# Linear attention's running state in a fused attention, FFN and expert kernel: summed in SBUF by VectorE, or summed in PSUM from keys that are scaled beforehand

## The chip, the cores and the metric

The kernel runs on one core of one Trainium2 chip. Its time is device microseconds from launch to end; the lower the better. Three runs of the kernel before gave 433.2, 433.91 and 435.3 us, median 433.91.

## The reference

Three stages follow one another, for two batches of 768 tokens. The first is attention with a decaying state, per batch and for each of 8 heads of 64 columns:

```
gamma[h] = 1 - 2 ** (-5 - h)
state = gamma * state + outer(k[t], v[t])        # 64 x 64 per head
y[t]  = q[t] @ state / 8
```

The second stage is a gated FFN with a convolution over three tokens (512 to 1024 to 512 columns). The third routes every token to one of 8 experts and applies that expert's two matrices. All of it is float32.

## The kernel before

Attention works on chunks of 128 tokens, six per head (`NCH = 6`, chunks 0 to 5), and on two heads at a time. Such a pair is a `Head` object: j = 0 lies on partitions 0 to 63, j = 1 on 64 to 127. There are 8 pairs, 0 to 7, so 48 steps. The order of instructions is the order of the Python program on each engine; no scheduler moves them.

One step calls `scores(c)` for one chunk and `output(c)` for the chunk two steps earlier. In TensorE's order a step is:

- `s_ps` (L279): the keys of the chunk against the queries of both heads; VectorE multiplies it by the decay mask into `at` (L281).
- `inc` (L287): keys times values of the chunk, 128 x 128, for chunks 0 to 4. It has one PSUM buffer. VectorE turns it into the next state `st` on the two diagonal 64 x 64 blocks: a copy for chunk 0 (L292), and for the others `new = gamma ** 128 * old + inc` (L294), one instruction per head.
- `y` (L297, L299): the chunk's own part from `at` and the values `vz`, and for chunks 1 to 5 the state's part, from `st` and the scaled queries. It has two PSUM buffers. ScalarE rounds `y` to the high part of `xT` (L301), VectorE writes the rest as the low part (L302), one step later.

Each float32 matmul is two instructions in the trace (x2). After these, `advance()` lets a few generators run one piece each on ScalarE, VectorE and GpSimd:

- `prepare()` of the next pair starts two steps after a pair's first: ScalarE copies the queries into `qz` (L250, two halves), GpSimd scales the queries in place (L253), ScalarE scales the keys in place by `gamma ** (127 - t)`, one instruction per head (L260), and copies the values into `vz` (L274). For pair 0, which is loaded and prepared in two parts, VectorE does one head's share (L248, L258).
- `convert()` turns the FFN's weights, which come as 64-bit words, into float32 high and low parts: L149 and L150 on VectorE, L151 on ScalarE, an add on GpSimd (L153), the high part on ScalarE (L171), the low part on GpSimd or VectorE (L173). For the second matrix it also transposes on TensorE and makes a small product (`wt`, `wc`, L186 to L192). A buffer of raw words comes free when L153 has read it; SyncE issues all loads in one queue (L143 for these words, L230 to L235 for a pair).

From step 25 on `ffn_in` slices (L133 to L135, 128 x 384) are put between attention's steps, 0.7 per step, and `hidden()` follows them on ScalarE and VectorE (L347 to L354). Attention takes from the start to about 90 us of the span; then come the rest of the FFN, the routing (about 210 to 240 us) and the experts.

Of the kernel before, what the change touches and what calls it, by code (L numbers as in the profile page):

```python
# [9 lines left out]
F32 = mybir.dt.float32  # L10
# [13 lines left out]
P = 128  # L24
CH = 128
# [16 lines left out]
A_COLS = 3 * CH + 2  # L42
# [12 lines left out]
def constants():  # L55
# [4 lines left out]
    for h in range(H):  # L60
        c, j = a[:, h // 2], h % 2
        c[:, C_DM + j * CH:C_DM + (j + 1) * CH] = np.where(d >= 0, 0.125 * g[h] ** np.maximum(d, 0), 0.0)
        c[:, C_KD + j] = g[h] ** (CH - 1 - t)
        c[64 * j:64 * j + 64, C_QD:C_QD + CH] = 0.125 * g[h] ** (t + 1)
# [27 lines left out]
def tile_kernel(ctx, tc, cat, cst, qT, kT, kN, vN, w_in, conv_w, w_out, wg, w1, w2, out):  # L92
# [125 lines left out]
    class Head:  # L218
# [21 lines left out]
        def prepare(self):  # L240
            hp = self.hp
            qd = ca[:, hp, C_QD:C_QD + CH]
            for c in self.parts:
                t = slice(c.start * CH, c.stop * CH)
                for j in range(2):
# [5 lines left out]
                    yield 1  # L251
                q1 = self.q1[:, c.start:c.stop]
                po.tensor_tensor(out=q1, in0=q1, in1=qd.unsqueeze(1).to_broadcast([P, len(c), CH]), op=ALU.mult)  # L253
                for j in range(2):
                    k1 = self.kv[:, 0, c.start:c.stop, 64 * j:64 * j + 64]
                    kd = ca[:, hp, C_KD + j:C_KD + j + 1]
                    if len(self.parts) > 1 and j:
                        ve.tensor_scalar(out=k1, in0=k1, scalar1=kd, scalar2=None, op0=ALU.mult)  # L258
                    else:
                        se.activation(out=k1, in_=k1, func=AF.Copy, scale=kd)  # L260
                    if len(self.parts) > 1:
                        self.values(c, j)
                    yield 1

            if len(self.parts) == 1:
                yield 1
                for c in (range(3), range(3, 6)):
                    for j in range(2):
                        self.values(c, j)
                    yield 3  # L270
# [12 lines left out]
        def output(self, c):  # L283
            at = self.at.pop(c)
            if c + 1 < NCH:
                inc = ps1.tile([P, P], F32, tag="i", name="inc", bufs=1)
                te.matmul(inc, self.kv[:, 0, c, :], self.kv[:, 1, c, :], start=True, stop=True)  # L287
                old, new = self.st[c % 2], self.st[(c + 1) % 2]
                for j in range(2):
                    pj = slice(64 * j, 64 * j + 64)  # L290
                    if c == 0:
                        ve.tensor_copy(out=new[pj, pj], in_=inc[pj, pj])  # L292
                    else:
                        ve.scalar_tensor_tensor(out=new[pj, pj], in0=old[pj, pj], scalar=self.g[j] ** CH, in1=inc[pj, pj], op0=ALU.mult, op1=ALU.add)  # L294
# [765 lines left out]
```

## Time and profile before

| | us |
|---|---|
| median of three runs | 433.91 |
| the profiled execution | 433.53 |
| its span, first to last instruction | 431.8 |
| TensorE busy in the span | 406.7 (94%) |
| VectorE busy | 290.1 (67%) |
| ScalarE busy | 259.4 (60%) |
| GpSimd busy | 91.6 (21%) |

Times in rows are microseconds from the start of the span. PE is TensorE, PEld its weight loads, DVE is VectorE, ACT is ScalarE, POOL is GpSimd, SP is SyncE. "x2" behind a row of the timeline means that two such instructions follow one another and are merged. What stands in brackets behind a row is the engine's idle time before it, and what ended that.

### The profile page before, as it was taken

The page shows a single profiled execution, that of the slowest core. Times are in us where ns is not written, and L with a number is a line of the kernel's source. Part 1 is how long each engine was busy: PE and PEld are TensorE (multiplying, and loading weights), DVE is VectorE, ACT ScalarE, POOL GpSimd, SP SyncE. Part 2 cuts the span into 40 slices and gives each one's busy share as a digit, 9 for nine tenths or more (in the row PEclk, how much of TensorE's full clock was granted, in tenths as well). Part 3 has the DMA queues.
Part 4 walks back from the last instruction along what each step waited for, and adds up shares of the span by engine and source line. Part 5 has one row for each costly group of instructions (what it writes and reads, how often), then busy time and mean ns, then how long its engine had stood idle before and what let it go on. Part 6 is the DMA issues. An engine that isn't in the chain of part 4 may idle for free.

```text
span 431.8 us, 7294 instructions
## 1 busy us (share of the span) xinstructions
PE 406.7 (94%) x2412; PEld 327.2 (76%) x2412; DVE 290.1 (67%) x518; ACT 259.4 (60%) x429; POOL 91.6 (21%) x92
## 2 busy tenths in 40 slices
PE   8898999997999999999999899999989999999991
PEld 7787897896898778989768676867738676776881
DVE  3798789798766350477899057968663796858650
ACT  2787677666755212566604166869555786958560
POOL 5256664213000000000000330205212132111210
PEclk9999999999999999999999999999999999999997
DMA  7989773320000101000296999999979999675001
GB/s 239 380 289 399 257 218 87 96 92 1 2 2 0 49 29 46 26 0 2 82 355 214 358 382 350 347 385 407 379 272 330 393 367 362 266 257 205 34 26 37
DMA packets 27324, 86.59 MB, mean 201 GB/s; under 512 B 3598, under 2 KB 4622, under 8 KB 27280
## 3 DMA queue, kind: packets, MB, share of 16 engines
q1 hardware_dynamic: 25200, 79.76, 50.6%
q0 software_dynamic: 2080, 6.29, 3.8%
q8 instruction: 21, 0.34, 0.3%
q14 instruction: 23, 0.19, 0.1%
HBM read 105.18 MB, written 6.55 MB: 259 GB/s over the span
## 4 chain that ended last, share of the span: by engine, by line
PE 35%; issue 26%; DMA 18%; DVE 14%; ACT 3%; POOL 2%; SPq 0%; POOLq 0%; DVEq 0%
DMA out_dram<-yo,it 15%; PE h_ps L133 5%; PE h_ps L135 4%; PE h_ps L134 4%; PE x_ps L133 4%; PE x_ps L134 3%; PE x_ps L135 3%; PE y L297 3%; PE s_ps L279 3%; DVE cc L350 2%; DMA kv<-in_kN_dram 2%; DVE na L149 2%; PE inc L287 2%; DVE na L150 1%; PE y L299 1%
## 5 line engine op out<-in xcount | busy, mean ns | idle before, releaser
L133 PE MATMUL h_ps<-xT,wih 128*128 128x384 f32 x128 | 46.5, 363 | 2.3 <-ACT wc L192 2.3
L350 DVE SCALAR_TENSOR_TENSOR cc<-h,cw,cc 128x768 f32<-128x768 f32 x32 | 35.1, 1097 | 16.8 <-ACT cc L347 16.8
L860 POOL DMA_INDIRECT out_dram<-yo,it x13 | 16.7, 1283 | 137.1 <-ACT yo L859 137.1
L724 POOL DMA_INDIRECT xg<-xs,it x13 | 18.8, 1442 | 125.5 <-DMA qc<-in_w_dram 118.6
L134 PE MATMUL h_ps<-xT,wih 128*128 128x384 f32 x128 | 43.1, 337 | 0.0
L135 PE MATMUL h_ps<-xT,wil 128*128 128x384 f32 x128 | 43.1, 336 | 0.0
L133 PE MATMUL x_ps<-woh,hg 128*128 128x512 f32 x96 | 38.5, 401 | 0.0
L134 PE MATMUL x_ps<-wol,hg 128*128 128x512 f32 x96 | 37.5, 391 | 0.0
L135 PE MATMUL x_ps<-woh,hg 128*128 128x512 f32 x96 | 37.5, 390 | 0.0
L715 DVE TENSOR_TENSOR ws0l<-r,ws0l 128x1024 fp32r<-128x1024 f32 x22 | 26.0, 1222 | 16.3 <-ACT ws0l L714 16.1
L297 PE MATMUL y<-at,vz 128*128 128x128 f32 x192 | 30.6, 281 | 1.7 <-DMA kv<-in_kN_dram 0.9
L715 DVE TENSOR_TENSOR ws0h<-r,ws0h 128x1024 fp32r<-128x1024 f32 x22 | 26.0, 1222 | 8.3 <-ACT ws0h L714 8.2
L715 DVE TENSOR_TENSOR wc<-r,wc 128x1024 fp32r<-128x1024 f32 x22 | 25.9, 1221 | 7.9 <-ACT wc L714 7.9
L714 ACT ACTIVATE ws0l<-r 128x1024 fp32r<-128x1024 f32 x22 | 22.1, 1052 | 13.6 <-PE y L135 13.6
L153 POOL TENSOR_TENSOR na<-na,raw 128x512 int32<-128x512 int32 (+1 forms) x17 | 21.9, 1290 | 38.2 <-DVE na L150 12.6
L715 DVE TENSOR_TENSOR ws1h<-r,ws1h 128x1024 fp32r<-128x1024 f32 x22 | 26.0, 1222 | 6.0 <-ACT ws1h L714 4.0
L279 PE MATMUL s_ps<-qz,kq 128*128 128x256 f32 x96 | 29.0, 384 | 1.0 <-DVE qz L248 1.0
L714 ACT ACTIVATE wc<-r 128x1024 fp32r<-128x1024 f32 x22 | 22.1, 1054 | 11.3 <-PE g L135 11.3
L297 PEld LDWEIGHTS y<-at,vz 128*128 128x128 f32 x192 | 25.3, 191 | 4.3 <-DVE xT L302 2.3
L133 PEld LDWEIGHTS h_ps<-xT,wih 128*128 128x128 f32 x128 | 24.1, 188 | 5.5 <-ACT wc L192 2.6
L281 DVE TENSOR_TENSOR at<-s_ps,ca 128x256 f32<-128x256 f32 x48 | 20.2, 420 | 11.6 <-PE s_ps L279 11.5
L486 ACT ACTIVATE xn<-x_ps 128x512 f32<-128x512 f32 x10 | 6.0, 599 | 32.8 <-PE x_ps L135 15.5
(231 smaller groups left out, 1041.5 us busy)
## 6 DMA issues: line engine op xcount, KB each, us to landing
r<-in_w_dram SPq DMA_DIRECT2D x88, 512.0 KB
qc<-in_w_dram SPq DMA_DIRECT2D x32, 512.0 KB
qs1l<-in_w_dram SPq DMA_DIRECT2D x32, 512.0 KB
raw<-in_w_in_dram SPq DMA_DIRECT2D x8, 512.0 KB
raw<-in_w_out_dram SPq DMA_DIRECT2D x8, 512.0 KB
kq<-in_qT_dram SPq DMA_DIRECT2D x7, 384.0 KB
kq<-in_kT_dram SPq DMA_DIRECT2D x7, 384.0 KB
kv<-in_vN_dram SPq DMA_DIRECT2D x7, 384.0 KB
```

The lines of the kernel that those rows point to most:

```text
L133: te.matmul(ps, lhi, rhi, start=first, stop=False)
L134: te.matmul(ps, lhi, rlo, start=False, stop=False)
L135: te.matmul(ps, llo, rhi, start=False, stop=last)
L153: po.tensor_tensor(out=a, in0=a, in1=lo, op=ALU.add)
L279: te.matmul(ps, self.kq[:, 0, tok], self.qz[:, :, tok], start=True, stop=True)
L281: ve.tensor_tensor(out=self.at[c], in0=ps, in1=self.dm, op=ALU.mult)
L297: te.matmul(y, vz[:, c, j, :], at[:, j, :], start=(j == 0), stop=(c == 0 and j == 1))
L350: ve.scalar_tensor_tensor(out=cc, in0=h[:, i:i + S], scalar=cw[:, m, i:i + 1], in1=cc, op0=ALU.mult, op1=ALU.add)
L714: se.activation(out=w[:, 0, h, :], in_=r, func=AF.Copy)
L715: ve.tensor_tensor(out=w[:, 1, h, :], in0=r, in1=w[:, 0, h, :].bitcast(F32), op=ALU.subtract)
L724: return po.indirect_dma_start(out=xg, out_offset=None, in_=xs[0:n], in_offset=bass.IndirectOffsetOnAxis(ap=it[:, j:j + 1], axis=0), bound ...
L860: po.indirect_dma_start(out=out, out_offset=bass.IndirectOffsetOnAxis(ap=it[:, j:j + 1], axis=0), in_=yo, in_offset=None, bounds_check=NT ...
```

## The change

The decay between chunks is moved from the state into the keys. The factor of a key becomes `gamma ** (127 - t + 128 * (4 - n))` for chunk n of 0 to 4, so that the plain sum of the chunks' `inc` products is the state, up to the factor `gamma ** (128 * (c + 1 - 5))` after chunk c.

- The keys of all five chunks and both heads are scaled by one GpSimd multiplication (128 x 640, its second operand a table broadcast over each head's 64 columns), ahead of the scaling of the queries. The last chunk's keys are no longer scaled. The two ScalarE instructions per pair (L260), and VectorE's two for pair 0 (L258), are gone. The table grows from 386 to 394 columns.
- `inc` is one PSUM tile per pair to which every chunk's product is added (`start=(c == 0)`).
- After each product ScalarE copies the first head's block of the sum into `st` times its factor, and VectorE the second head's. The two VectorE instructions (L292, L294) are gone.

```diff
--- before.py
+++ after.py
@@ -39,7 +39,8 @@
 
 
 C_DM, C_QD, C_KD = 0, 2 * CH, 3 * CH
-A_COLS = 3 * CH + 2
+NST = NCH - 1
+A_COLS = 3 * CH + 2 * NST
 
 C_ID = 0
 C_S0 = C_ID + P
@@ -60,7 +61,8 @@
     for h in range(H):
         c, j = a[:, h // 2], h % 2
         c[:, C_DM + j * CH:C_DM + (j + 1) * CH] = np.where(d >= 0, 0.125 * g[h] ** np.maximum(d, 0), 0.0)
-        c[:, C_KD + j] = g[h] ** (CH - 1 - t)
+        for n in range(NST):
+            c[:, C_KD + 2 * n + j] = g[h] ** (CH - 1 - t + CH * (NST - 1 - n))
         c[64 * j:64 * j + 64, C_QD:C_QD + CH] = 0.125 * g[h] ** (t + 1)
     c = np.zeros((P, C_COLS))
     e = np.arange(E)
@@ -249,21 +251,20 @@
                     else:
                         se.activation(out=self.qz[pj, j, t], in_=self.kq[pj, 1, t], func=AF.Copy)
                     yield 1
+                n = min(c.stop, NST)
+                k1 = self.kv[:, 0, c.start:n, :].rearrange("p c (j d) -> p (c j) d", j=2)
+                kd = ca[:, hp, C_KD + 2 * c.start:C_KD + 2 * n].unsqueeze(2).to_broadcast([P, 2 * (n - c.start), D])
+                po.tensor_tensor(out=k1, in0=k1, in1=kd, op=ALU.mult)
                 q1 = self.q1[:, c.start:c.stop]
                 po.tensor_tensor(out=q1, in0=q1, in1=qd.unsqueeze(1).to_broadcast([P, len(c), CH]), op=ALU.mult)
-                for j in range(2):
-                    k1 = self.kv[:, 0, c.start:c.stop, 64 * j:64 * j + 64]
-                    kd = ca[:, hp, C_KD + j:C_KD + j + 1]
-                    if len(self.parts) > 1 and j:
-                        ve.tensor_scalar(out=k1, in0=k1, scalar1=kd, scalar2=None, op0=ALU.mult)
-                    else:
-                        se.activation(out=k1, in_=k1, func=AF.Copy, scale=kd)
-                    if len(self.parts) > 1:
+                if len(self.parts) > 1:
+                    for j in range(2):
                         self.values(c, j)
+                        yield 1
+
+            if len(self.parts) == 1:
+                for _ in range(3):
                     yield 1
-
-            if len(self.parts) == 1:
-                yield 1
                 for c in (range(3), range(3, 6)):
                     for j in range(2):
                         self.values(c, j)
@@ -283,15 +284,13 @@
         def output(self, c):
             at = self.at.pop(c)
             if c + 1 < NCH:
-                inc = ps1.tile([P, P], F32, tag="i", name="inc", bufs=1)
-                te.matmul(inc, self.kv[:, 0, c, :], self.kv[:, 1, c, :], start=True, stop=True)
-                old, new = self.st[c % 2], self.st[(c + 1) % 2]
-                for j in range(2):
-                    pj = slice(64 * j, 64 * j + 64)
-                    if c == 0:
-                        ve.tensor_copy(out=new[pj, pj], in_=inc[pj, pj])
-                    else:
-                        ve.scalar_tensor_tensor(out=new[pj, pj], in0=old[pj, pj], scalar=self.g[j] ** CH, in1=inc[pj, pj], op0=ALU.mult, op1=ALU.add)
+                if c == 0:
+                    self.sum = ps1.tile([P, P], F32, tag="i", name="inc", bufs=1)
+                te.matmul(self.sum, self.kv[:, 0, c, :], self.kv[:, 1, c, :], start=(c == 0), stop=True, skip_group_check=True)
+                new = self.st[(c + 1) % 2]
+                d = [g ** (CH * (c + 1 - NST)) for g in self.g]
+                se.activation(out=new[0:64, 0:64], in_=self.sum[0:64, 0:64], func=AF.Copy, scale=d[0])
+                ve.tensor_scalar(out=new[64:128, 64:128], in0=self.sum[64:128, 64:128], scalar1=d[1], scalar2=None, op0=ALU.mult)
             y = ps1.tile([P, CH], F32, tag="y", name="y")
             for j in range(2):
                 te.matmul(y, vz[:, c, j, :], at[:, j, :], start=(j == 0), stop=(c == 0 and j == 1))
```

TensorE's order is the same in both programs. Three places in the order of the other engines follow; line numbers are each program's own, and the brackets name the engines and DMA queues whose semaphores an instruction waits for.

First, ScalarE where pair 3 begins: high part of pair 2's last chunk, a weight conversion (`wih`, `raw`) and the queries of pair 4 (`qz_104`). In the kernel before these rows stand there:

```order
L311 ACTIVATE cw<-na 128x24 [waits Pool_49]
L301 ACTIVATE xT<-y 128x128 [waits PE_49]
L171 ACTIVATE wih<-na 128x512 [waits Pool_49]
L151 ACTIVATE raw<-raw 128x512 [waits DMAHW6_49,DVE_49,Activation_49]
L250 ACTIVATE qz_104<-kq 64x768 [waits DMAHW7_49]
L301 ACTIVATE xT<-y 128x128 [waits PE_49]
L250 ACTIVATE qz_104<-kq 64x768
```

Here no copy into the state is ScalarE's. In the changed kernel ScalarE has these rows there:

```order
L310 ACTIVATE cw<-na 128x24 [waits Pool_49]
L300 ACTIVATE xT<-y 128x128 [waits PE_49]
L173 ACTIVATE wih<-na 128x512 [waits Pool_49]
L153 ACTIVATE raw<-raw 128x512 [waits DMAHW6_49]
L252 ACTIVATE qz_104<-kq 64x768 [waits DMAHW7_49]
L292 ACTIVATE st_110<-inc 64x64 [waits PE_49]
L300 ACTIVATE xT<-y 128x128 [waits PE_49]
L252 ACTIVATE qz_104<-kq 64x768
```

The copies of `inc` into `st` stand behind the conversion and the queries and ahead of the high parts.

The rows of VectorE at the same place in the kernel before, with the conversion (`na`) and the masked scores (`at`):

```order
L313 CAST sel<-cs 40x10
L281 TENSOR_TENSOR at<-s_ps,ca 128x256 [waits PE_49]
L302 TENSOR_TENSOR xT<-y,xT 128x128 [waits Activation_49]
L149 TENSOR_SCALAR na<-raw 128x512 [waits DMAHW6_49,Pool_49]
L150 SCALAR_TENSOR_TENSOR na<-raw,na 128x512 [waits DVE_49]
L281 TENSOR_TENSOR at<-s_ps,ca 128x256 [waits PE_49]
L292 COPY st_110<-inc 64x64 [waits PE_49]
L292 COPY st_110<-inc 64x64
```

Here two copies follow `at`, one per head, and wait for TensorE alone. In the changed kernel VectorE has these:

```order
L312 CAST sel<-cs 40x10
L282 TENSOR_TENSOR at<-s_ps,ca 128x256 [waits PE_49]
L301 TENSOR_TENSOR xT<-y,xT 128x128 [waits Activation_49]
L151 TENSOR_SCALAR na<-raw 128x512 [waits DMAHW6_49,Pool_49]
L152 SCALAR_TENSOR_TENSOR na<-raw,na 128x512 [waits DVE_49]
L282 TENSOR_TENSOR at<-s_ps,ca 128x256 [waits PE_49]
L293 TENSOR_SCALAR st_110<-inc 64x64 [waits Activation_49]
```

The copy of the sum (`st<-inc`) waits for ScalarE, where the copies before waited for TensorE; behind it stand the low part (`xT`) and the next `at`.

Second, ScalarE where pair 7 begins, around the table load for the sigmoid (`cc`). In the kernel before:

```order
L352 ACT_TABLE_LOAD
L352 ACTIVATE cc<-cc 128x768 [waits DVE_49]
L301 ACTIVATE xT<-y 128x128 [waits PE_49]
L186 ACTIVATE wt<-wt_ps 128x512 [waits Pool_49]
L171 ACTIVATE woh<-na 128x512 [waits Pool_49]
L301 ACTIVATE xT<-y 128x128 [waits PE_49] x2
```

Here the high parts of pair 6's last chunk and of pair 7's first two chunks follow with nothing of the state between them. In the changed kernel ScalarE has these:

```order
L351 ACT_TABLE_LOAD
L351 ACTIVATE cc<-cc 128x768
L300 ACTIVATE xT<-y 128x128 [waits PE_49]
L188 ACTIVATE wt<-wt_ps 128x512 [waits Pool_49]
L173 ACTIVATE woh<-na 128x512 [waits Pool_49]
L292 ACTIVATE st_110<-inc 64x64 [waits PE_49]
L300 ACTIVATE xT<-y 128x128 [waits PE_49]
L292 ACTIVATE st_109<-inc 64x64 [waits PE_49]
L300 ACTIVATE xT<-y 128x128 [waits PE_49]
```

The first copy of pair 7 stands behind the table load, the sigmoid, a high part and two pieces of the conversion (`wt`, `woh`).

Third, GpSimd in pairs 1 and 2: the queries (`kq`) of pairs 2 and 3, low parts of weights (`wil`) and the conversion's adds (`na`). In the kernel before:

```order
L253 TENSOR_TENSOR kq<-kq,ca 128x768 [waits DMAHW4_49,DMAHW2_49,Activation_49]
L173 TENSOR_TENSOR wil<-na,wih 128x512 [waits Activation_49]
L153 TENSOR_TENSOR na<-na,raw 128x512 [waits DMAHW7_49,DVE_49,Activation_49]
L253 TENSOR_TENSOR kq<-kq,ca 128x768 [waits DMAHW1_49,DMAHW0_49,DMAHW3_49,PE_49,Activation_49]
L153 TENSOR_TENSOR na<-na,raw 128x24 [waits DMAHW0_49,DVE_49,Activation_49]
```

Here GpSimd scales queries alone. In the changed kernel GpSimd has these:

```order
L257 TENSOR_TENSOR kv<-kv,ca 128x640 [waits DMAHW6_49,DMAHW4_49]
L259 TENSOR_TENSOR kq<-kq,ca 128x768 [waits DMAHW2_49,Activation_49]
L175 TENSOR_TENSOR wil<-na,wih 128x512 [waits Activation_49]
L155 TENSOR_TENSOR na<-na,raw 128x512 [waits DMAHW7_49,DVE_49,Activation_49]
L257 TENSOR_TENSOR kv<-kv,ca 128x640 [waits DMAHW5_49,DMAHW3_49,PE_49]
L259 TENSOR_TENSOR kq<-kq,ca 128x768 [waits DMAHW1_49,Activation_49]
L155 TENSOR_TENSOR na<-na,raw 128x24 [waits DMAHW0_49,DVE_49,Activation_49]
```

A multiplication of the keys (`kv`, for pairs 2 and 3) that waits for a load stands directly ahead of the queries' one each time.

## Rows read from the trace of the kernel before

**Rows 1.** Windows: length, busy us (count) by engine, PEclk, DMA share, GB/s
```profile
15.00:90.00 75.00, 70.33 (x486) 63.63 (x486) 62.96 (x196) 54.33 (x136) 36.29 (x28) 1.00 0.67 232
```
**Rows 2.** Waits of TensorE, 15 to 90 us: total us, times, longest
```profile
PE inc L287 <- DVE st L294: 2.8, 3, 1.6
PE y L297 <- DVE xT L302: 0.6, 2, 0.4
...
PE inc L287 <- DVE st L292: 0.5, 2, 0.3
```
**Rows 3.** Groups by shape, 0 to 100 us: busy us, mean ns | idle before
```profile
L294 DVE SCALAR_TENSOR_TENSOR st<-st,inc 64x64 f32<-64x64 f32 x64 | 13.7, 215 | 1.7 <-PE inc L287 0.9
L301 ACT ACTIVATE xT<-y 128x128 fp32r<-128x128 f32 x48 | 13.2, 274 | 19.6 <-PE y L299 17.6 <-PE y L297 1.5
...
L253 POOL TENSOR_TENSOR kq<-kq,ca 128x768 f32<-128x768 f32 x7 | 11.7, 1665 | 11.6 <-ACT qz L250 8.2 <-DVE at L281 2.2 <-DVE st L294 1.2
...
L260 ACT ACTIVATE kv<-kv,ca 128x384 f32<-128x384 f32 x14 | 8.5, 606 | 0.2 <-DMA kv<-in_kN_dram 0.2
...
L292 DVE COPY st<-inc 64x64 f32<-64x64 f32 x16 | 3.5, 216 | 0.1
...
L253 POOL TENSOR_TENSOR kq<-kq,ca 128x512 f32<-128x512 f32 x1 | 1.3, 1267 | 3.9 <-DVE qz L248 3.9
...
L192 ACT ACTIVATE wc<-wc_ps 128x9 f32<-128x9 f32 x2 | 0.3, 170 | 0.0
```
**Rows 4.** Timeline, 10 to 13 us, ScalarE: start, us, instruction [idle before]
```profile
11.02 0.85 ACT L250 ACTIVATE qz<-kq 64x768 f32<-64x768 f32 x1 [2.98 <-DMA kq<-in_qT_dram]
```
**Rows 5.** Timeline, 35 to 40 us, pair 3's first step
```profile
36.93 0.28 ACT L301 ACTIVATE xT<-y 128x128 fp32r<-128x128 f32 x1 [0.37 <-PE y L299]
...
38.63 0.46 PE L287 MATMUL inc<-kv 128*128 128x128 f32 x2 [0.20 <-DVE st L292]
...
38.93 0.25 ACT L301 ACTIVATE xT<-y 128x128 fp32r<-128x128 f32 x1
```
**Rows 6.** Timeline, 76 to 82 us, pair 7's first step
```profile
76.64 0.28 ACT L301 ACTIVATE xT<-y 128x128 fp32r<-128x128 f32 x1 [1.93 <-PE y L299]
...
80.67 0.71 PE L297 MATMUL y<-at,vz 128*128 128x128 f32 x4
81.19 0.28 ACT L301 ACTIVATE xT<-y 128x128 fp32r<-128x128 f32 x1
```
**Rows 7.** Timeline, 28 to 34 us, the conversion in pair 2
```profile
29.69 1.54 POOL L253 TENSOR_TENSOR kq<-kq,ca 128x768 f32<-128x768 f32 x1 [1.18 <-DVE st L294]
...
29.93 1.59 DVE L149 TENSOR_SCALAR na<-raw 128x512 int32<-128x512 int32 x1
...
31.55 0.69 DVE L150 SCALAR_TENSOR_TENSOR na<-raw,na 128x512 int32<-128x512 int32 x1
...
32.49 0.44 DVE L294 SCALAR_TENSOR_TENSOR st<-st,inc 64x64 f32<-64x64 f32 x2
...
33.08 0.46 PE L287 MATMUL inc<-kv 128*128 128x128 f32 x2 [1.56 <-DVE st L294]
```
**Rows 8.** Timeline: two issues of keys (SPq L235) and one landing
```profile
7.41 0.33 SPq L235 DMA_DIRECT2D kv<-in_kN_dram  x1
...
14.56 0.62 ACT L260 ACTIVATE kv<-kv,ca 128x384 f32<-128x384 f32 x1 [0.22 <-DMA kv<-in_kN_dram]
...
23.05 0.44 SPq L235 DMA_DIRECT2D kv<-in_kN_dram  x1
```
**Rows 9.** Timeline, 40 to 44 and 72 to 76 us, GpSimd and VectorE
```profile
40.28 1.83 POOL L253 TENSOR_TENSOR kq<-kq,ca 128x768 f32<-128x768 f32 x1
...
41.31 1.09 DVE L149 TENSOR_SCALAR na<-raw 128x512 int32<-128x512 int32 x1
...
72.46 1.30 POOL L153 TENSOR_TENSOR na<-na,raw 128x512 int32<-128x512 int32 x1 [1.14 <-ACT vz L274]
...
73.26 1.32 DVE L350 SCALAR_TENSOR_TENSOR cc<-h,cw,cc 128x768 f32<-128x768 f32 x1
```

## The prediction

> **What bounds the kernel now.** The page's slices come first: TensorE is busy from end to end, so a change in attention counts only as far as TensorE is held there. The windows say how much that is: between 15 and 90 us TensorE is idle 75 − 70.33 = 4.7 us; VectorE is the next busiest with 62.96 us, ScalarE has 54.33, GpSimd 36.29, and the granted clock is 1.00 [rows 1]. The waits name who holds TensorE: VectorE, for 2.8 + 0.6 + 0.5 = 3.9 us, most of it the state's instructions; ScalarE almost never [rows 2]. The timeline, read at the places where `inc` waits, then shows what VectorE was doing: in pair 2 its shift L149 took 1.59 us beside GpSimd's multiplication, L150 followed, and `inc` started at 33.08 after 1.56 us of idle TensorE [rows 7]. So the stage is TensorE's, with VectorE's queue as the thing that breaks its step.
>
> **What goes and what comes.**
> VectorE loses 64 instructions of 215 ns and 16 of 216 ns, 17.2 us, and gets 40 back that also read 64 columns of PSUM; at 216 ns they are 8.6 us [rows 3]. It is 8.6 us lighter.
> ScalarE loses 14 x 606 ns = 8.5 us and the two short ones of pair 0. It gets 40 copies of 64 columns from PSUM. No row shows one; nine columns take 170 ns and 128 take 274 [rows 3], so a copy lies between, and I take 220 ns, 8.8 us. Its busy time stays.
> GpSimd gets, for each of seven pairs, 640 columns: between the 1.27 us of 512 and the 1.67 us of 768 [rows 3]; I take 1.5, some 11 us in all with pair 0. The operand broadcast along the columns is in no row; at worst it doubles this.
> The loads grow by 8 columns in 386 of one small table: nothing.
>
> What decides is not the load but the order. ScalarE is served in order, and its copy stands behind whatever `advance()` gave it in the step before. VectorE's copy waits for ScalarE's, by the order shown. The next `inc` writes the tile that both read, so it waits for both. From the time f at which ScalarE comes to its copy, the next `inc` can start at f + 0.22 (ScalarE) + 0.22 (VectorE) + 0.2 for two hand-overs: VectorE's state instructions of 32.49 end at 32.93 and `inc` starts at 33.08, 0.15 later [rows 7]; the one from ScalarE to VectorE I set at 0.05. So at f + 0.65. Behind the waiting copy VectorE holds a low part, which frees a `y` buffer, and the next `at`.
> Between one `inc` and the next stand TensorE's other matmuls of the step, so a ScalarE that is free when `inc` ends costs nothing. It is late only at the turn from one pair to the next, where query copies of 0.83 us and conversions meet. I went through all seven turns; these are late.
>
> - *Start.* The first copy stands behind the queries of pair 1, which wait for their load until 11.02 and take 0.85 [rows 4]. The second `inc` is about 1.5 us late. ScalarE loses a key instruction right behind, and the values on which TensorE waits next come when they came: 0, between −0.3 and +0.4.
> - *Pair 2, 28 to 33 us.* VectorE reaches L149 earlier, the keys' multiplication comes first and the queries' after it. If VectorE gets L149 and L150 in before them, up to 1.2 us of the 1.56 [rows 7] is gained; if L150 falls behind the keys, 0.3 is lost. I take −0.3.
> - *Pair 3.* ScalarE has a high part, two conversions and the queries from 36.93 on without a pause, and is free at 38.93; so f = 38.93 and `inc` starts at 39.6, where it started at 38.63 [rows 5]: +0.9, between 0.5 (faster hand-overs) and 1.0. Two steps on L149, which took 1.09 at 41.31 behind the 1.83 us multiplication from 40.28 [rows 9], finds two multiplications there instead of one: +0.3, between 0 and 1.5.
> - *Pair 7.* From 76.64 ScalarE works through a conversion, values, a table load, the sigmoid and two more conversions, and reaches the high part of pair 7's first chunk at 81.19. That is f for the first copy. `inc` starts at 81.85 and `y` behind it, where `y` started at 80.67 [rows 6]: 1.2 and a part of the 0.46 that an `inc` takes [rows 5], +1.3, between 0.9 and 1.5.
> - *Pairs 5 and 6.* Here steps are longer by an FFN slice, ScalarE is in time, and VectorE's lead of one state instruction per step shortens the smaller waits of [rows 2]: −0.5, between −0.8 and 0.
>
> Sum: 0 − 0.3 + 0.9 + 0.3 + 1.3 − 0.5 = +1.7 us. What follows attention depends on its end: the FFN's rest, routing and the experts' loads, whose buffers come free then. So the shift is carried to the end. The profiled execution is 433.5 us (span 431.8), which makes 435.2; it lies 0.4 us under the median, and I set 435.4 for a median. The bounds of the terms add up to −0.9 and +4.7, from 432.8 to 438.4 on the same footing (433.7 for no shift).
>
> **The skill against the rows.** Both L149, beside a GpSimd instruction that began before it, and L350 from 73.26, beside one from 72.46 to 73.76, end late: L149 about 0.3 after GpSimd's end, L350 about 0.8 after it, as if each had begun only then [rows 7, 9]. The Trainium skill says so (SBUF — State Buffer, "Who interferes with whom"): VectorE and GpSimd share one pair of ports, held for a whole instruction, by VectorE in its fast two-port mode and against GpSimd's reads also with two SBUF inputs. The rows agree. L150 and L350 have two such inputs. By this rule each microsecond given to GpSimd is one in which the conversion can be shut out, and it speaks against this change. What that would make of the time is the third rival, which stands on rows alone.
>
> **Rivals.**
> - *The exchange is hidden.* ScalarE's lateness is taken up by the idle time before its high parts, 17.6 us in 24 waits [rows 3], and VectorE's gains make up for the rest: 433.9. Against it: that idle time lies inside steps, not at the turns.
> - *VectorE's relief decides.* All 3.9 us of TensorE's waits for VectorE go [rows 2] and ScalarE is never later than VectorE was: 433.9 − 3.9 = 430.0. For it: 8.6 us less on the engine that holds TensorE. Against it: the wait for ScalarE gives VectorE a new reason to stand still at the turns.
> - *GpSimd shuts the conversion out.* Place: pair 2 at 30 us. A pair's keys came 14.56 − 7.41 = 7.15 us after their issue, and pair 3's are issued at 23.05 [rows 8], so by this estimate they land at 30.2. GpSimd, idle until then, multiplies keys until 31.7 and queries until 33.3; if L150 gets its turn only then, it ends at 34.0, and `at` and the copy bring `inc` to 34.8 instead of 33.08: +1.7. With pairs 3 and 7 (+2.5) and no gains: 433.7 + 4.2 = 437.9 (+2.5 is 0.9 + 0.3 + 1.3). It decides from the point where the second multiplication starts ahead of L150. Against it: L149 arrives at about 30.1, perhaps just ahead of the keys.
>
> **How the numbers follow.** What a measurement of this kernel can tell from no change is about 0.5%, 2.2 us. Forecast 0.47, its own range 433.5 to 437 (0.36 of it within 0.5%, 0.11 above); hidden 0.12, all within; VectorE's relief 0.15 (0.13 faster, 0.02 within); GpSimd 0.26, slower. That makes faster 0.13, the same 0.50, slower 0.37. The range reaches from near half-way between the hidden case and the second rival, 432.2, to the third, 438.0.
>
> **What would show it.** L292 of the changed kernel on ScalarE near 220 ns, 40 times, and L293 on VectorE ended by ScalarE in the waits; `inc` (L289) waiting about 0.9 us at pair 3's and 1.3 at pair 7's second chunk, for VectorE by name and ScalarE behind it; L257 on GpSimd 1.5 us and idle before pair 3's until its keys land; attention's last `y` one to two us later, and the end as much. It is wrong if `inc` does not wait at those two places, if attention ends earlier, or if GpSimd's new instruction takes 3 us.

## The result and the profile after

The changed kernel takes 436.09 us (median of 6 runs, 434.98 to 437.36) where the kernel before, run beside it, takes 433.56 (6 runs, 432.93 to 435.3): a ratio of 1.0059, 95% interval 1.0032 to 1.0087. The forecast was 435.4 in a range of 432.2 to 438.0. The time lies in the range and 0.7 us above the forecast; by the median the change is slower by a little more than what can be told from no change. Ratios here and below leave out slow runs, those more than 1.5% above the fastest of their kernel: two of the twelve with both copies on VectorE, its profiled one among them, and one in each of two series of the kernel before.

The profiled execution of the changed kernel took 434.98 us, with a span of 433.1. The windows of attention, beside [rows 1] (busy time of TensorE, its weight loads, VectorE, ScalarE and GpSimd; the granted clock; the DMA share and rate):

```profile
15.00:90.00 75.00, 68.44 (x469) 61.69 (x468) 56.83 (x154) 52.16 (x154) 46.62 (x35) 1.00 0.66 229
```

VectorE is 6.1 us lighter and GpSimd 10.3 us heavier, as the change says, and TensorE has become idler, from 4.7 to 6.6 us. TensorE's waits in the same stretch (total, times, longest), beside [rows 2]:

```profile
PE inc L289 <- DVE st L293: 5.4, 5, 1.6
...
PE y L296 <- DVE xT L301: 0.3, 1, 0.3
```

The waits for VectorE by name have grown from 3.9 to 5.7 us, though VectorE does less. The groups by shape, 0 to 100 us (busy time, mean ns, and idle time before them), beside [rows 3]:

```profile
L257 POOL TENSOR_TENSOR kv<-kv,ca 128x640 f32<-128x640 f32 x7 | 9.5, 1361 | 3.8 <-DMA kv<-in_kN_dram 3.3 <-PE inc L289 0.5
L293 DVE TENSOR_SCALAR st<-inc 64x64 f32<-64x64 f32 x40 | 9.1, 228 | 12.6 <-ACT st L292 11.9
L292 ACT ACTIVATE st<-inc 64x64 f32<-64x64 f32 x40 | 8.5, 212 | 9.0 <-PE inc L289 8.9
```

The prices were right: 1.36 us for the keys (1.5 was taken, and the doubling that was allowed for the broadcast operand did not come), 212 and 228 ns for the copies (220 and 216). The order is what shows in the last column: VectorE's copy stood still for 11.9 us in all because ScalarE's had not come. I measure attention's end by the start of its last high part on ScalarE: 89.97 us before, 93.35 after, so +3.4 us, twice the +1.7 of the sum:

```profile
89.97 0.28 ACT L301 ACTIVATE xT<-y 128x128 fp32r<-128x128 f32 x1 [0.38 <-PE y L299]
93.35 0.28 ACT L300 ACTIVATE xT<-y 128x128 fp32r<-128x128 f32 x1 [0.61 <-PE y L298]
```

The places follow, in order of time (start us, us, instruction, idle time before it). How late attention is at a chunk is read from the start of the chunk's high part, beside the same one before.

The start, on ScalarE, beside [rows 4]:

```profile
11.52 0.84 ACT L252 ACTIVATE qz<-kq 64x768 f32<-64x768 f32 x1 [2.70 <-DMA kq<-in_qT_dram]
12.27 0.20 ACT L292 ACTIVATE st<-inc 64x64 f32<-64x64 f32 x1
```

The first copy does stand behind the queries, and these waited for a load that landed 0.5 us later than before; attention is 0.5 us late from here, 0.7 at the end of pair 1. The 0.2 us of pair 1 is ScalarE's: its copy for the pair's second chunk stands behind the second half of the queries and starts at 22.01, and VectorE's, at 22.26, has waited 0.54 us for it. No term of the sum has this place.

The conversion in pair 2, on GpSimd, VectorE and TensorE, beside [rows 7]:

```profile
29.73 1.26 POOL L257 TENSOR_TENSOR kv<-kv,ca 128x640 f32<-128x640 f32 x1 [0.51 <-PE inc L289]
...
30.58 0.23 DVE L293 TENSOR_SCALAR st<-inc 64x64 f32<-64x64 f32 x1 [0.53 <-ACT st L292]
...
30.94 1.54 POOL L259 TENSOR_TENSOR kq<-kq,ca 128x768 f32<-128x768 f32 x1
31.04 1.72 DVE L151 TENSOR_SCALAR na<-raw 128x512 int32<-128x512 int32 x1
32.80 0.69 DVE L152 SCALAR_TENSOR_TENSOR na<-raw,na 128x512 int32<-128x512 int32 x1
...
34.14 0.49 PE L289 MATMUL inc<-kv 128*128 128x128 f32 x2 [1.59 <-DVE st L293]
```

VectorE reaches the shift 1.1 us later than before (31.04 for 29.93), after a copy that waited 0.53 us for ScalarE, and 0.1 us after the second multiplication has begun. The shift takes 1.72 us, and ends 0.28 after GpSimd does.

Pair 3: the turn, and two steps on the conversion behind GpSimd, beside [rows 5, 9]:

```profile
39.16 0.84 ACT L252 ACTIVATE qz<-kq 64x768 f32<-64x768 f32 x1
39.90 0.21 ACT L292 ACTIVATE st<-inc 64x64 f32<-64x64 f32 x1
...
40.14 0.23 DVE L293 TENSOR_SCALAR st<-inc 64x64 f32<-64x64 f32 x1 [0.93 <-ACT st L292]
...
40.42 0.49 PE L289 MATMUL inc<-kv 128*128 128x128 f32 x2 [1.02 <-DVE st L293]
...
42.46 1.82 POOL L259 TENSOR_TENSOR kq<-kq,ca 128x768 f32<-128x768 f32 x1
...
43.23 1.34 DVE L151 TENSOR_SCALAR na<-raw 128x512 int32<-128x512 int32 x1
...
45.94 0.49 PE L289 MATMUL inc<-kv 128*128 128x128 f32 x2 [1.18 <-DVE st L293]
```

ScalarE comes to its copy at 39.90, VectorE follows at 40.14, `inc` at 40.42: 0.52 us from one to the other, where 0.65 was taken (the two hand-overs took 0.03 and 0.05 us, where 0.05 and 0.15 were taken). The wait names VectorE; the row above it shows that VectorE itself waited for ScalarE. Pair 7, beside [rows 6], is the same picture:

```profile
82.99 0.21 ACT L292 ACTIVATE st<-inc 64x64 f32<-64x64 f32 x1
...
83.23 0.23 DVE L293 TENSOR_SCALAR st<-inc 64x64 f32<-64x64 f32 x1 [1.79 <-ACT st L292]
...
83.52 0.49 PE L289 MATMUL inc<-kv 128*128 128x128 f32 x2 [1.43 <-DVE st L293]
```

The last 0.2 of the 3.4 us falls at attention's last chunk, which no term of the sum has either. ScalarE's copy stands behind a 0.93 us piece of the FFN's convolution (`cc`), VectorE's copy waits for it, and behind that stands the low part for which `y` waits. The first row is the kernel before, the others the changed kernel:

```profile
88.99 0.71 PE L297 MATMUL y<-at,vz 128*128 128x128 f32 x4 [0.21 <-DVE xT L302]
```

```profile
91.56 0.20 ACT L292 ACTIVATE st<-inc 64x64 f32<-64x64 f32 x1
91.79 0.23 DVE L293 TENSOR_SCALAR st<-inc 64x64 f32<-64x64 f32 x1 [1.10 <-ACT st L292]
...
92.38 0.71 PE L296 MATMUL y<-at,vz 128*128 128x128 f32 x4 [0.45 <-DVE xT L301]
```

Attention ends 3.4 us late and the span is only 1.3 us longer. What gives 2 us back, and why the median says 2.5, was open; so was how much of the +3.4 is ScalarE's and how much GpSimd's.

### The profile page after: what moved, and what is told of

It reads as the page before. It is cut to its first block, busy times and chain, and to the rows that moved or that the text cites. A ratio compares the mean times of both kernels' runs of the same rounds, so it can differ in the third digit from the quotient of the medians.

```text
span 433.1 us, 7237 instructions
## 1 busy us (share of the span) xinstructions
PE 407.4 (94%) x2412; PEld 327.2 (76%) x2412; DVE 284.7 (66%) x476; ACT 258.6 (60%) x453; POOL 101.9 (24%) x101
## 4 chain that ended last, share of the span: by engine, by line
PE 35%; issue 26%; DMA 17%; DVE 13%; ACT 5%; POOL 2%; SPq 1%; POOLq 0%; DVEq 0%
DMA out_dram<-yo,it 15%; PE h_ps L135 4%; PE h_ps L136 4%; PE h_ps L137 4%; PE x_ps L135 4%; PE y L296 4%; PE x_ps L137 3%; PE x_ps L136 3%; PE s_ps L280 3%; DVE cc L349 3%; PE inc L289 2%; DVE na L151 2%; DMA kq<-in_qT_dram 2%; PE y L298 1%; DVE na L152 1%
```

## The experiments

Theory S (A in the first runs): ScalarE's late copies are what costs. Theory G (B there): GpSimd's multiplication of the keys, which shuts VectorE's conversion out. All ratios are to the kernel before, run beside each kernel. "End" is attention's last high part in the profiled execution (before 89.97). "Lost" is the time at full clock that TensorE lost to stretches at 1.2 GHz before that end, summed over the windows from 10 to 92.5 us as length times (1 − granted clock). How much of it reaches the end is an estimate; in the one place where it can be seen, 1.6 of 1.7 us did: from pair 7's `inc` to the end the changed kernel took 9.8 us in its first execution (83.52 to 93.35), and 11.5 in its second (83.05 to 94.51), where the clock fell in between.

| kernel | ratio, 95% interval | end us | lost us | end less lost |
|---|---|---|---|---|
| changed kernel | 1.0059 (1.0032–1.0087) | 93.35 | 0 | 93.35 |
| changed, again | 1.0035 (1.0004–1.0065) | 94.51 | 1.7 | 92.8 |
| both copies on VectorE | 1.0001 (0.9964–1.0037) | 96.32 | 5.1 | 91.2 |
| GpSimd's keys alone | 1.0020 (0.9989–1.0050) | 91.47 | 1.7 | 89.8 |
| VectorE's copy first | 1.0083 (1.0049–1.0116) | 93.60 | 1.7 | 91.9 |
| first chunk on VectorE | 1.0041 (1.0011–1.0071) | 93.22 | 1.7 | 91.5 |
| no keys' multiplication | – | 91.48 | 0 | 91.48 |
| both multiplications in pieces | 1.0096 (1.0061–1.0131) | 95.70 | 1.7 | 94.0 |
| before, queries in pieces | 0.9974 (0.9944–1.0004) | 89.11 | 0 | 89.11 |
| masked copy | 0.9952 (0.9930–0.9974) | 88.60 | 0 | 88.60 |
| masked, keys on ScalarE | 1.0029 (0.9996–1.0062) | 90.23 | 0 | 90.23 |
| the same, queries in pieces | 0.9986 (0.9960–1.0012) | 90.21 | 1.7 | 88.5 |
| masked, queries in pieces | 0.9985 (0.9960–1.0009) | 89.00 | 0 | 89.00 |

**Both copies on VectorE.**

```diff
-se.activation(out=new[0:64, 0:64], in_=self.sum[0:64, 0:64], func=AF.Copy, scale=d[0])
+ve.tensor_scalar(out=new[0:64, 0:64], in0=self.sum[0:64, 0:64], scalar1=d[0], scalar2=None, op0=ALU.mult)
```

> Both heads' copies of the sum stand on VectorE; ScalarE has none; all else as in the changed kernel. The measure is the start of attention's last high part on ScalarE (before 89.97 us, changed kernel 93.35, so +3.4). Theory A (at the turns from pair to pair the copy on ScalarE comes late, and inc waits for it): the three shifts made there go, 0.5 at the start, 0.6 in pair 3, 1.25 in pair 7; what stays is GpSimd's part, 0.5 in pair 2 and 0.35 in pair 3. Last high part at about 91.0 (+1.0), time about 434.3. Theory B (GpSimd's multiplication of the keys shuts VectorE out, and that is most of it): last high part still at +2.5 to +3.4, time 435.5 to 436. Theory C (VectorE's relief is what counts, so 8.6 us more on it costs): above 93.4, time over 436.

The time is what theory S gave, 433.9 us beside 434.1, ratio 1.0001 (theory G's 435.5 lies just inside the interval's upper end); pairs 3 and 7 lose nothing at their turns. The profiled execution (438.69 us, far above its median) shows something else. In pair 2 VectorE comes late, and the conversion's second instruction falls behind the second multiplication; TensorE waits 2.35 us, and then its clock is down (VectorE, TensorE, and two windows):

```profile
32.73 1.92 DVE L152 SCALAR_TENSOR_TENSOR na<-raw,na 128x512 int32<-128x512 int32 x1
...
35.40 0.80 PE L289 MATMUL inc<-kv 128*128 128x128 f32 x2 [2.35 <-DVE st L293]
```

```profile
32.50:35.00 2.50, 0.55 (x4) 0.15 (x2) 2.47 (x4) 0.95 (x3) 2.46 (x3) 1.00 1.02 404
35.00:37.50 2.50, 2.10 (x9) 2.10 (x10) 1.69 (x7) 0.00 (x0) 2.29 (x2) 0.58 1.00 378
```

This happens three times in that execution and costs 1.7 us each time. Less that loss the end would lie at 91.2, near theory S's 91.0.

**GpSimd's part alone.** The keys' multiplication on GpSimd as in the change, with `g[h] ** (CH - 1 - t)` in the table; the recurrence of before on VectorE.

> GpSimd's part of the change alone: the keys are scaled on GpSimd (with the factor of the kernel before, the same in each chunk), the state is kept on VectorE by the two recurrence instructions of before. Theory A: only the conversion's delays in pairs 2 and 3 are left, +0.5 and +0.35, less something for the 8.5 us that ScalarE loses: last high part at 90.5 to 91.0, time about 434. Theory B: +2.5 to +3.4, time 435.5 to 436.

Less the fall of the clock, the end comes 0.2 us *before* that of the kernel before. Here VectorE was in time in pair 2, a microsecond ahead of the keys (VectorE and GpSimd):

```profile
29.61 0.42 DVE L151 TENSOR_SCALAR na<-raw 128x512 int32<-128x512 int32 x1
30.06 0.69 DVE L152 SCALAR_TENSOR_TENSOR na<-raw,na 128x512 int32<-128x512 int32 x1
...
30.59 1.28 POOL L257 TENSOR_TENSOR kv<-kv,ca 128x640 f32<-128x640 f32 x1 [2.40 <-DMA kv<-in_kN_dram]
```

That took 1.2 us out of pair 2. Pair 3 lost 3.0 in its place, 1.7 of it by the clock, which fell in a wait of 1.57 us for `inc` at 39.44; there VectorE's shift stood behind another instruction of GpSimd, the conversion's own subtraction. So in this execution GpSimd's extra work cost nothing but the clock: what the multiplication does hangs on which of two instructions comes first. The time does not bear this out as well as the trace: the median is 435.33 us, near theory G's 435.5 and not theory S's 434, though the ratio's interval holds 1.

**VectorE's copy first.** The two copies change places in the program.

> The changed kernel with VectorE's copy written ahead of ScalarE's, so that ScalarE waits for VectorE and no longer VectorE for ScalarE; inc still waits for both. Theory A1 (what costs is that inc waits for a late ScalarE): about 0.2 us less at each late turn, last high part at 92.6 to 93.1, time about 435.5. Theory A2 (what costs is that VectorE stands still behind ScalarE, with low parts and at queued behind it): last high part at 91.5 or earlier, time about 434.5.

Net of the clock the end (91.9) lies between the two expectations, and the time, 437.3 us, is above both: nothing is gained by letting VectorE go first. Here too VectorE reached pair 2's shift ahead of the keys (29.18 for 29.63), the pair ended 2.1 us ahead of the kernel before, and in pair 3 all of it was gone again. Which of the two forms holds is not settled.

**First chunk on VectorE.**

```diff
+if c == 0:
+    ve.tensor_scalar(out=new[0:64, 0:64], in0=self.sum[0:64, 0:64], scalar1=d[0], scalar2=None, op0=ALU.mult)
+else:
-se.activation(out=new[0:64, 0:64], in_=self.sum[0:64, 0:64], func=AF.Copy, scale=d[0])
+    se.activation(out=new[0:64, 0:64], in_=self.sum[0:64, 0:64], func=AF.Copy, scale=d[0])
```

> The changed kernel with the copies of a pair's first chunk both on VectorE (8 of 40); the other 32 stay split. Theory A: the late copies are those of the first chunk; without them the 0.5 + 0.6 + 1.25 us go and the last high part comes at about 91.0, time about 434.3, as if all copies were on VectorE. Rival (ScalarE's lateness at the turn is only handed on): the second chunk's copy is late in its place, half or more of the shift stays, last high part at 92.2 or later, time about 435.2.

Pair 7's turn loses nothing now; the end less the clock's loss is 91.5, nearer to theory S than to its rival. The time does not show it: 1.0041 lies between the two ratios of the changed kernel. In the profiled execution a conversion behind GpSimd in pair 2 (1.94 us of wait) and the clock behind it took it back; that the other runs lost it there too is not shown.

**No multiplication of the keys.** The line `po.tensor_tensor(out=k1, in0=k1, in1=kd, op=ALU.mult)` goes.

> The changed kernel without GpSimd's multiplication of the keys (the keys go into the sum unscaled, so that part of the computation is left out); the split copies stay. Theory S (ScalarE's late copies at the turns are what costs): the shifts at the start, in pair 3 and in pair 7 stay (0.5 + 0.6 + 1.25), those behind GpSimd go; attention's last high part at about 92.2 us (before 89.97, changed kernel 93.35), time about 435.5. Theory G (the keys' multiplication is what costs, by shutting VectorE's conversion out): last high part at 91 or earlier, time about 434. [...]

Read to attention's end only: with unscaled keys the stages behind compute on other numbers and take longer (469.46 us in all, ratio 1.0792). The end is 91.48, between theory S's 92.2 and theory G's 91: +1.5 us is left without the keys. All of it is ScalarE's and comes at the end of attention, 1.25 us at pair 7's turn and 0.2 at the last chunk; what the start and pair 1 lost, 0.45, is down to 0.04 by the end of pair 2. The other 1.9 us of the 3.4 go with the keys' multiplication in this pair of executions, 0.25 of them with a load at the start that landed earlier here. Pair 3's turn, 0.6, is there too, but what it lost was made good two steps on, where the conversion now came through. Pair 7's wait is there to the hundredth (TensorE):

```profile
81.64 0.49 PE L288 MATMUL inc<-kv 128*128 128x128 f32 x2 [1.43 <-DVE st L292]
```

**The changed kernel again**, to see what repeats.

> The changed kernel unchanged, once more, for a second profiled execution and a second ratio. The profiled execution before had attention's last high part 3.4 us after that of the kernel before, and its span only 1.3 us longer, while the medians are 2.5 us apart. Theory S (late ScalarE copies) says that the waits at the start, in pair 3 and in pair 7 come again at the same places with the same lengths to 0.2 us, since they follow from the order of instructions. Theory G says that the waits behind GpSimd (pairs 2 and 3) come at other lengths, since they depend on when a load lands, and that the granted clock falls in some executions: last high part anywhere from 92.5 to 96, time about 436.

Each expectation held in part. ScalarE's waits came again, as theory S has it, 1.02 us in pair 3 and, in pair 7 (TensorE):

```profile
83.05 0.49 PE L289 MATMUL inc<-kv 128*128 128x128 f32 x2 [1.43 <-DVE st L293]
```

The shift at the start did not: the queries' load landed at 11.01 us, as before the change, and pair 0 ends level with that of the kernel before. So that 0.5 us was the load's, not the order's: over the 14 profiled executions of all kernels ScalarE begins these queries between 10.58 and 11.52 us, and the first execution of the changed kernel is the latest. The waits behind GpSimd did not come at other lengths, as theory G had it: 1.61 us in pair 2 and 1.19 in pair 3, for 1.59 and 1.18. In pair 2 it was now the conversion's second instruction that GpSimd shut out (GpSimd, VectorE):

```profile
30.73 1.73 POOL L259 TENSOR_TENSOR kq<-kq,ca 128x768 f32<-128x768 f32 x1
...
31.09 1.92 DVE L152 SCALAR_TENSOR_TENSOR na<-raw,na 128x512 int32<-128x512 int32 x1
```

Less the fall of the clock the end is +2.8 us against the kernel before; that of the first execution is +2.9 less its late load. And the clock fell behind pair 7's wait, where it had not in the first execution. The window behind that wait, here and then in the first execution:

```profile
86.00:88.50 2.50, 2.50 (x12) 2.30 (x10) 0.97 (x4) 0.22 (x1) 1.28 (x1) 0.55 0.00 0
```

```profile
86.00:88.50 2.50, 1.97 (x17) 1.76 (x15) 1.45 (x4) 1.23 (x5) 1.28 (x1) 1.00 0.00 0
```

**Both multiplications in pieces.** One GpSimd instruction per chunk, `for i in range(c.start, n)` for the keys and `for i in c` for the queries.

> The changed kernel with GpSimd's two multiplications of a pair cut into one instruction per chunk (5 for the keys, 6 for the queries, of 128 columns; GpSimd needs perhaps 4.5 us for a pair in place of 3.1); the split copies stay. Theory G: VectorE's two conversion instructions come in between two pieces and take at most 0.5 us longer than alone (0.42 and 0.69), where the long multiplications made them 1.3 to 2.2; last high part at 92.3 (the turns' 2.35 us stay), time about 435. Theory S alone: the conversion gains, but attention's end stays at 92.5 to 93.5. Rival: the pieces shut VectorE out again and again and its two instructions still end with the last piece, or GpSimd is late with the keys: 93.5 or later, time over 436.

The rival was right in the end and the time. On GpSimd, 0 to 95 us:

```profile
L260 POOL TENSOR_TENSOR kq<-kq,ca 128x128 f32<-128x128 f32 x48 | 21.8, 489 | 1.6 <-DMA kv<-in_vN_dram 1.6
...
L258 POOL TENSOR_TENSOR kv<-kv,ca 128x128 f32<-128x128 f32 x40 | 15.4, 419 | 7.0 <-DMA kv<-in_kN_dram 6.4 <-PE s_ps L281 0.5
```

A pair takes 6 x 489 + 5 x 419 = 5.0 us of GpSimd in place of 3.0. In pair 2 the pieces do what theory G hoped for: the conversion's two instructions take 0.68 and 0.78 us (from 30.81 and 31.52), and the pair loses nothing against the kernel before. What is lost is lost behind another instruction of GpSimd, a low part of the weights (L175), here where pair 3 begins (GpSimd, VectorE, TensorE):

```profile
37.58 1.29 POOL L175 TENSOR_TENSOR wil<-na,wih 128x512 fp32r<-128x512 f32 x1 [0.86 <-ACT wih L173]
37.77 1.66 DVE L152 SCALAR_TENSOR_TENSOR na<-raw,na 128x512 int32<-128x512 int32 x1
...
40.17 0.46 PE L290 MATMUL inc<-kv 128*128 128x128 f32 x2 [1.50 <-DVE st L294]
```

The same two meet again at 56.50, also for 1.66 us. That GpSimd's longer queue is what brings them together was not tested.

**The kernel before, queries in pieces.**

> The kernel before with only the multiplication of a pair's queries on GpSimd cut into one instruction per chunk (6 of 128 columns). Theory G: the conversion in pair 2, which took 1.59 us behind that multiplication and held TensorE for 1.56, takes about 0.5; last high part 0.8 to 1.5 us before that of the kernel before (89.97), so 88.5 to 89.2, time 432 to 433. Rival (other waits take its place, or the pieces shut VectorE out as long): 89.5 to 91, time 434 or more.

With the queries' multiplication alone the end is 0.9 us earlier in pieces, and in pair 2 (GpSimd, VectorE)

```profile
29.54 2.90 POOL L253 TENSOR_TENSOR kq<-kq,ca 128x128 f32<-128x128 f32 x6 [1.15 <-DVE st L294]
29.77 0.46 DVE L149 TENSOR_SCALAR na<-raw 128x512 int32<-128x512 int32 x1
30.27 0.79 DVE L150 SCALAR_TENSOR_TENSOR na<-raw,na 128x512 int32<-128x512 int32 x1
```

the shift that took 1.59 us in [rows 7] takes 0.46, and both instructions run among the pieces. The ratio, 0.9974, still holds 1 in its interval.

**The masked copy.**

```diff
-se.activation(out=new[0:64, 0:64], in_=self.sum[0:64, 0:64], func=AF.Copy, scale=d[0])
-ve.tensor_scalar(out=new[64:128, 64:128], in0=self.sum[64:128, 64:128], scalar1=d[1], scalar2=None, op0=ALU.mult)
+d = ca[:, self.hp, C_SD + c:C_SD + c + 1]
+ve.scalar_tensor_tensor(out=new, in0=self.sum, scalar=d, in1=mask, op0=ALU.mult, op1=ALU.mult)
```

The mask takes the place of one of the four state tiles; the other three go round.

> The sum is copied by one VectorE instruction of 128 columns, scaled by a column of a table and multiplied by a 0/1 mask; ScalarE copies nothing, GpSimd's multiplication of the keys stays. VectorE then has 40 instructions of about 0.30 us (12 us) for the state, where before had 17.2 and the copies both on VectorE 17.2. Theory S: no late copy at a turn, last high part at 90.5 or earlier, time 433 to 434. Theory G: what decides is whether the conversion falls behind a multiplication of GpSimd, in pair 2 or 3 or 4; it does so here too, at another place than in the other kernels: a wait of TensorE of 1.5 us or more, last high part at 91.5 or later, time 434 to 436.

This one beats both kernels: 432.3 us beside 434.64, ratio 0.9952, with an interval wholly under 1 and under those of the changed kernel, and the end at 88.60. Its state costs VectorE 13.7 us, where before it took [rows 3]'s 13.7 and 3.5 for the 16 short ones (0 to 100 us):

```profile
L297 DVE SCALAR_TENSOR_TENSOR st<-inc,ca,st 128x128 f32<-128x128 f32 x40 | 13.7, 342 | 1.0 <-PE inc L294 0.8
```

VectorE has 3.5 us less to do, its state waits for TensorE alone, and it comes early: at pair 2's shift at 28.96, 0.15 us ahead of the keys. It is not free of theory G: in pair 3 the conversion's second instruction takes 2.18 us behind GpSimd, and `inc` waits 1.86 us; the clock stayed up there.

**Masked, keys on ScalarE**, ten instructions of 64 columns a pair; then the same with the queries in pieces.

> The masked copy (one VectorE instruction of 128 columns per state) with the keys scaled on ScalarE, chunk by chunk and head by head: 10 instructions of 64 columns per pair in place of the two of 606 ns of the kernel before; GpSimd keeps only the queries' multiplication. Theory G (with GpSimd's keys gone the conversion is shut out less): no wait of 1.5 us or more in pairs 2 to 4, last high part at 88 or earlier, against 88.60 with the keys on GpSimd, time 431 to 432. Theory S (ScalarE's load at the turns counts): 10 instructions of about 0.2 us are 2 us of ScalarE for a pair; the high part that stands behind them is late by up to 1 us a turn, last high part at 90 or later, time over 434.

> As the kernel with the masked copy and the keys on ScalarE, and the queries' multiplication on GpSimd cut into one instruction per chunk, as in the kernel before with pieces, where VectorE's first conversion instruction fell from 0.6 to 0.45 us in the mean. If the two gains add up: last high part 0.5 to 1 us before that kernel's, time 430 to 431. Rival: the pieces (489 ns each beside VectorE) keep GpSimd's queue longer, so that its additions for the conversion come later; no gain or a loss of 0.5 us.

The end and the time are theory S's: 90.23, and 435.5 us (part of the time may be the clock's: the mean granted clock of its twelve runs, 0.986, is the lowest but for the kernel with unscaled keys). My price was off (0 to 95 us):

```profile
L266 ACT ACTIVATE kv<-kv,ca 128x64 f32<-128x64 f32 x80 | 21.4, 339 | 3.0 <-DMA kv<-in_kN_dram 3.0
```

339 ns, not 200; the values that stand behind them hold TensorE for 1.9 us in two waits. With the queries in pieces the longest wait for VectorE falls from 1.4 to 0.4 us, and the ratio from 1.0029 to 0.9986; the clock fell early, behind the wait for the values at the start. Less that the end is 88.5, by this estimate 1.7 us before the kernel without pieces; the 430 to 431 us that were expected did not come (433.15).

**Masked, queries in pieces.**

> The masked copy with the keys' multiplication whole on GpSimd and the queries' cut into one instruction per chunk. Theory G: in the kernel with the masked copy inc still waits 3.7 us in pairs 0 to 7 for VectorE (longest 1.9), where the conversion stands behind GpSimd; behind the whole keys' multiplication VectorE gets in between two pieces, the longest wait falls under 1.3, last high part at 87.5 to 88.3 against 88.60, time 431 to 432. Rival: a pair's pieces and the keys make 4.2 us of GpSimd in place of 3.1 and hold VectorE longer in sum: last high part at 89 or later, time 433 or more.

The longest wait is 1.4 us and not 1.9, but the end is 0.4 us later than without pieces: the rival. In time it can't be told from the masked copy.

## Why the prediction held, and where it did not

- *What bounds attention* was read rightly: TensorE's turn, broken by VectorE's queue. So was what would replace that wait. `inc` waits at both named places, for VectorE by name and ScalarE behind it.
- *Pair 7*: +1.3 forecast, +1.25 measured, in both executions. *Pair 3*: +0.9 and +0.3 forecast, +0.6 and +0.35 measured. *Pairs 5 and 6*: −0.5 forecast, −0.3 and −0.2 over the two pairs in the two executions (−0.5 as far as pair 6's third chunk, of which 0.3 comes back by its end).
- *The start* was 0, as forecast, once the load landed as before; the +0.5 of the first execution is that load's.
- *The step that failed is pair 2*: "VectorE reaches L149 earlier", −0.3. It reaches the conversion later, 31.04 or 30.54 instead of 29.93, since its copy waits for ScalarE, which is busy with the queries. I had looked for ScalarE's lateness only at the turns where it holds `inc`; one that only shifts VectorE by half a microsecond decides which engine comes first, the conversion or the second multiplication. The conversion came second, and pair 2 lost 0.3 us against pair 1's end in both executions. The third rival named place and mechanism rightly; its price, +1.7, was too high. GpSimd's two multiplications ended at 32.48 and not at 33.3, since the keys landed earlier than its 30.2 and were scaled faster, so `inc` came at 34.14 (33.65 in the second execution) and not at 34.8.
- *Two places are missing*: "It is late only at the turn from one pair to the next" does not hold. ScalarE's copy is late inside pair 1 and at the last chunk too, +0.2 us each in both executions.
- *The sum* is then 0.2 + 0.3 + 0.6 + 0.35 − 0.25 + 1.25 + 0.2 = 2.65 us. With small remainders at other chunks that is the 2.8 and 2.9 us that the two executions show less the late load and the clock, where 1.7 was forecast. That the time came out 0.7 us from the forecast is therefore luck in part: what follows attention varies by more than that, as the last point says.
- *A step that is missing*: the sum counts what TensorE waits, not that its clock can fall behind a wait. Each fall in these traces cost 1.7 us more, as much as the whole sum. It came behind the same wait of 1.43 us in one execution and not in the other, so it is no term but a chance. The changed kernel has four waits above a microsecond between 15 and 90 us, the kernel before two (1.56 in [rows 7], and 1.08 at 43.96). That more such waits make falls more frequent is not what the runs show: the mean granted clock is 0.991 over the changed kernel's first six runs and 0.992 over its other twelve, and 0.990 over 103 runs of the kernel before. So the changed kernel's longer time is not the clock's.
- *"So the shift is carried to the end"* held on the whole, though the first pair of traces seemed to say otherwise. From attention's end to the end of the span the traces of all kernels but the one with unscaled keys took 339.1 to 342.9 us; the kernel before, with 341.8, is on the long side, the changed kernel with 339.8 and 341.0 on the short side and in the middle. The end of the span moves by 1.15 us for 1 us of attention's end (a line through the 13 traces). The 2 us "given back" lie within that spread, and no run shows them to be an effect of the change.

The Trainium skill's rule on the shared port pair (SBUF — State Buffer, "Who interferes with whom") is borne out further than I used it: the conversion's second instruction, with two SBUF inputs, takes 0.69 us when it does not have to wait for GpSimd and 1.92 behind L259. That the rule makes the loser wait for a whole instruction also says what pieces do, and the rows of pair 2 agree: the shift takes 0.46 us among the pieces of one multiplication and 0.68 among those of two, for 1.59 and 1.72 behind the whole ones.

That ScalarE's late copies and GpSimd's keys cost what TensorE waits in attention is shown place by place in two executions. How the change splits between the two is not settled. One pair of executions gives 1.5 us for ScalarE's copies and 1.9 for the keys and an earlier load; the time with both copies on VectorE is level with that of the kernel before, which speaks for ScalarE; the time with GpSimd's keys alone is 1.2 us longer, within what can be told from no change, which speaks for GpSimd. The parts depend on each other: without ScalarE's copies VectorE came ahead of the keys in one kernel, where they cost nothing in attention, and behind them in another (both copies on VectorE), where the end was 1.2 us late less the clock. A kernel in which VectorE's copy does not wait for ScalarE's at all, with the work still split, was not run.

## What to carry to other kernels

Splitting a small pair of copies between two engines saves 8 us of busy time and can still lose, when the second waits for the first and the first stands in a long queue; one masked instruction on the engine that already had the work saved 3.5 us of it and, with the keys left on GpSimd, gained 0.5%. Where two engines exclude each other, ask of each change who arrives first, to a tenth of a microsecond, before asking how much each has to do. And judge a few tenths of a per cent by many runs: one pair of traces showed +1.3 us, the medians +1.3 and +2.5.

## What the runs showed of the hardware that was not expected

- In 7 of 14 profiled executions the granted clock fell to 0.50 (1.2 GHz) in attention, once or more, at a cost of 1.7 us each: in or behind single waits of TensorE of 1.43 to 2.35 us, and twice at the start behind two waits close together (0.70 and 1.04; 0.77 and 1.12). Behind waits of 1.43, 1.56 and 1.86 us, and behind the same 0.77 and 1.12 (masked, keys on ScalarE), it stayed at 1.00 in other executions.
- GpSimd took 1.66 us for 768 columns in one instruction, and 6 x 489 ns = 2.9 us for the same columns in six.
- ScalarE took 212 ns for 64 columns out of PSUM with a constant factor, and 339 ns for 64 columns of SBUF in place with a factor per partition.
